# The last sums of a fused attention and feed-forward kernel: from GpSimd's only sum tile to VectorE and a tile of the scores' pool

## The chip, the cores and the metric

The kernel runs on one core of one Trainium2 chip. The metric is the device time of one execution in microseconds (us). The engines are called as the profile calls them: PE is TensorE (matmuls; PEld its weight loads), DVE is VectorE, ACT is ScalarE, POOL is GpSimd, and SP is the engine from whose queue most transfers (DMAs) are issued.

## The reference

```python
# q, k, v: (8, 8, 576, 64) float32; w_in: (512, 2048), w_out: (2048, 512)
scores = q @ k.transpose(0, 1, 3, 2) / sqrt(64)
kth = np.partition(scores, -32, axis=-1)[..., -32:-31]      # 32nd largest of each row
scores = np.where(scores >= kth, scores, -1e9)
attn = softmax(scores)                                       # over the last axis
x = (attn @ v).transpose(0, 2, 1, 3).reshape(4608, 512)
h = x @ w_in
out = (0.5 * h * (1 + erf(h / sqrt(2)))) @ w_out             # exact gelu
```

Attention with the 32 largest scores of each row kept, and a feed-forward layer with an exact gelu on the 4608 tokens that come out of it.

## The kernel before, in words

One program in float32 interleaves two stages, and the order of the instructions on every engine is written out by hand, as a loop over steps `n` with calls in a fixed order. An engine executes its instructions in that order. Semaphores are derived from which tile an instruction reads and writes, and from when a tile's slot was last used.

*Attention* works on 144 items of 128 rows by 1152 scores (two heads or halves of heads side by side). For an item, PE makes the scores (L370), ACT copies them into a tile of the scores' pool (tag `s`, six slots in turn), DVE finds the 32nd largest (L450, L453), ACT makes the exponentials (L495, L496), POOL divides by the sum (L507), PE turns the tile over (L553) and multiplies by `v` (L615). The result goes into `xT`.

*The feed-forward layer* works on "units": 256 tokens and two of the 16 blocks of 128 hidden columns (`FT` = 16). Units are taken in pairs, and `NU` is their number, so that `NU - 2` is the first unit of the last pair. For a pair, `first_block` makes `h` on PE (16 matmuls, L673), `gelus` applies the gelu on ACT into a tile `g` (L689, two slots), and `second_block` multiplies by `w_out`. Blocks are ordered so that `second_block` of a pair comes behind `first_block` of the next pair. At the end of the program no `first_block` is left, and so `second_block(NU - 4)` is followed at once by `second_block(NU - 2)`.

`second_block` is a product of 2 x 2 blocks made with seven multiplications instead of eight (the Strassen-Winograd scheme). It needs sums of the quarters of `g`, which `sums` makes: s1, s2 and s4 go into a tile `sum` that has one slot, and a third addition overwrites a quarter of `g` itself. The block starts with the seventh product (`seven_piece`, two matmuls, L809), whose operand is the quarter of `g` that the third addition has overwritten; then come three pairs of products, `TRIO = ((1, 2), (6, 5), (4, 3))`, 12 matmuls in all on L811 (four to a pair of products), which read `g`, `sum`, `w_out_sb` and `w_sum`. The seventh product is copied by ACT (L827, L830) and added up by POOL in `y7` (L832).

After the last block of a token group the products are combined into the output. For the last group of all, `last_parts` does so, called once after each pair of products (k = 0, 1, 2): for k = 0 ACT copies product 1 (L887); for k = 1 DVE makes five additions (L893 to L899) of which the second, L894, adds product 2 to product 1 and is stored at once (L895); for k = 2 come two more (L901, L903). Four stores of 128 x 256 float32 (128 KB) end the program: three on SP's queue (L895, L898, L902), one on ACT's (L904).

```python
dve(y0[:, B2], a[:, 0], y0[:, B1], op=add)                        # L893
dve(y0[:, B1], end_of["a"][:, 1], y0[:, B1], op=add)              # L894
nc.sync.dma_start(out=out[last_row : last_row + P, B1], in_=y0[:, B1])
dve(s7, s7, y0[:, B2], op=add)                                    # L896
```

`part_tile()` gives one of three slots of 128 x 256 float32, which the group before uses as well.

Of the kernel before, what the change touches and what calls it, by code (L numbers as in the profile page):

```python
# [14 lines left out]
def kernel(  # L15
# [19 lines left out]
    nc = tc.nc  # L35
    f32, i32, u32 = mybir.dt.float32, mybir.dt.int32, mybir.dt.uint32
    bf16, i16, u16 = mybir.dt.bfloat16, mybir.dt.int16, mybir.dt.uint16
    AF = mybir.ActivationFunctionType
    ALU = mybir.AluOpType

    B, H, S, D = q.shape
    P = 128
# [20 lines left out]
    work = ctx.enter_context(tc.tile_pool(name="work", bufs=2))  # L63
# [589 lines left out]
    NU = len(units)  # L653
    B1, B2 = slice(0, HALF), slice(HALF, DM)
# [43 lines left out]
    def sums(u):  # L698

        g = g_of[u].rearrange("p x (f n) -> p x f n", f=2)  # L700
        a11, a21, a12, a22 = (g[:, :, f, h * P : (h + 1) * P] for f in range(2) for h in range(2))
        t = work.tile([P, 2, 3, P], f32, tag="sum", bufs=1, name="sum")
        s1, s2, s4 = (t[:, :, x] for x in range(3))
        nc.gpsimd.tensor_tensor(s1, a21, a22, op=ALU.add)
        nc.gpsimd.tensor_tensor(s2, s1, a11, op=ALU.subtract)
        nc.gpsimd.tensor_tensor(a21, a11, a21, op=ALU.subtract)
        nc.gpsimd.tensor_tensor(s4, a12, s2, op=ALU.subtract)
        sums_of[u] = t

    def weight_sums(j):  # L710
# [29 lines left out]
    def y_tile():  # L740
        return work.tile([P, DM], f32, tag="y", name="y")

    def part_tile():
        return work.tile([P, HALF], f32, tag="part", bufs=3, name="part")
# [89 lines left out]
    end_of = {}  # L834

    def trio_piece(u, names, x):
# [8 lines left out]
        if u + x == NU - 1 or (end_of.get("last") and u + 2 == NU):  # L845
            last_parts(tok, k, a)
            return
# [34 lines left out]
    def last_parts(tok, k, a):  # L882

        dve, add = nc.vector.tensor_tensor, ALU.add
        if k == 0:
            end_of["y"] = y0, y1 = y_tile(), y_tile()
            nc.scalar.copy(out=y0[:, B1], in_=a[:, 0])  # L887
            end_of["a"] = a
            return
        y0, y1 = end_of["y"]  # L890
        s7 = y7[0]
        if k == 1:
            dve(y0[:, B2], a[:, 0], y0[:, B1], op=add)  # L893
            dve(y0[:, B1], end_of["a"][:, 1], y0[:, B1], op=add)  # L894
            nc.sync.dma_start(out=out[last_row : last_row + P, B1], in_=y0[:, B1])  # L895
            dve(s7, s7, y0[:, B2], op=add)  # L896
            dve(y1[:, B2], a[:, 1], s7, op=add)
            nc.sync.dma_start(out=out[last_row + P : last_row + 2 * P, B2], in_=y1[:, B2])  # L898
            dve(y0[:, B2], a[:, 1], y0[:, B2], op=add)  # L899
            return  # L900
        dve(y0[:, B2], a[:, 1], y0[:, B2], op=add)  # L901
        nc.sync.dma_start(out=out[last_row : last_row + P, B2], in_=y0[:, B2])  # L902
        dve(y1[:, B1], s7, a[:, 0], op=ALU.subtract)  # L903
        nc.scalar.dma_start(out=out[last_row + P : last_row + 2 * P, B1], in_=y1[:, B1])  # L904

    last_row = NT - TL - 2 * P
# [32 lines left out]
    def run_small(room):  # L939

        while summing:
            sums(summing.pop(0))
            room -= 4
        while small and room > 0:
            n, f = small.pop(0)
            f()
            room -= n
# [69 lines left out]
    first = {2: (0, 1, 1), 3: (2, 2, 3)}  # L1017
    prep_in, squares_in = {}, {}
    for pair in range(2, n_pairs):
        b, p = divmod(pair, NP)  # L1020
# [147 lines left out]
```

## Time and profile before

| | us |
|---|---|
| runs (three) | 1553.4, 1556.66, 1557.61 |
| median of the runs | 1556.66 |
| profiled execution, its own time | 1557.3 |
| span of the profiled execution, first to last instruction | 1555.5 |
| mean granted PE clock | 0.994 |

| engine | busy us | share of the span |
|---|---|---|
| PE | 1522.8 | 98% |
| DVE | 1330.3 | 86% |
| ACT | 1165.3 | 75% |
| POOL | 1141.5 | 73% |

All times in a trace count from the span's start. A line of the timeline gives the start, the duration (for a merged row of several instructions from the first start to the last end), the engine, the line of the kernel, and the tiles written and read; "[2.43 <-POOL g L706]" means that the engine stood idle for 2.43 us before it and that POOL's instruction on L706 ended that. The chain of waits is followed back from the last instruction, each step to what released it. The profile has two records for each of these float32 matmuls, so that `seven_piece` stands as x4 and a block's L811 as x24. The granted clock is the share of its full rate that PE was given in a window.

### The profile page before, as it was taken

What the parts mean: (1) busy time and instruction counts of PE and PEld (TensorE: products, weight loads), DVE (VectorE), ACT (ScalarE), POOL (GpSimd) and SP (SyncE); (2) the same over time, 40 slices, a digit from 0 to 9 for tenths busy, and PEclk for the clock granted to TensorE, in tenths of its full rate; (3) what the DMA queues carried; (4) which work ended last, traced back from release to release, by engine and by line L of the source; (5) the groups of instructions that cost most, each with busy time, mean ns of one, the idle gap of its engine ahead of it and who ended that gap; (6) DMA issues with size and microseconds to landing.
All of it is one profiled execution on the core that took longest, in us unless ns stands there. A gap on an engine that the chain in (4) does not pass through costs nothing. (4 is left out here: it accounts for less than half of the span.)

```text
span 1555.5 us, 28139 instructions
## 1 busy us (share of the span) xinstructions
PE 1522.8 (98%) x9280; PEld 1199.5 (77%) x9280; DVE 1330.3 (86%) x4571; ACT 1165.3 (75%) x2050; POOL 1141.5 (73%) x1291
## 2 busy tenths in 40 slices
PE   7899999999999999999999999999999999999998
PEld 5676578877777778887777778787877777787887
DVE  8998799989999988998989997988998998988700
ACT  6998877767777777777777778777777777777720
POOL 4886567767787868777787877776788786877632
PEclk9999999999999999999999999999999999999999
DMA  6513210012101111012201111002110111000000
GB/s 180 158 61 117 89 45 1 1 37 54 24 15 31 35 26 31 1 30 42 39 18 16 30 31 45 1 23 36 34 24 22 24 30 32 15 1 15 7 14 14
DMA packets 185298, 56.35 MB, mean 36 GB/s; under 512 B 176161, under 2 KB 176705, under 8 KB 185153
## 3 DMA queue, kind: packets, MB, share of 16 engines
q1 hardware_dynamic: 183888, 54.13, 14.6%
q8 instruction: 73, 1.20, 0.3%
q14 instruction: 73, 0.59, 0.1%
q10 hardware_dynamic: 1200, 0.39, 0.1%
q0 software_dynamic: 64, 0.03, 0.0%
HBM read 45.08 MB, written 9.44 MB: 35 GB/s over the span
## 5 line engine op out<-in xcount | busy, mean ns | idle before, releaser
L673 PE MATMUL h_ps<-xT,w_in_sb 128*128 128x256 f32 (+1 forms) x2560 | 541.4, 362 | 1.9 <-ACT xT L620 1.9
L673 PEld LDWEIGHTS h_ps<-xT,w_in_sb 128*128 128x128 f32 x2560 | 435.4, 191 | 73.4 <-issue 25.3
L450 DVE MAX8 top<-lists 128x8 f32<-128x288 f32 x792 | 321.1, 447 | 0.0
L507 POOL TENSOR_TENSOR s<-s,rden 128x1152 f32<-128x1152 f32 x144 | 302.7, 2102 | 0.3 <-DVE rden L482 0.3
L496 ACT ACTIVATE s<-s,bias 128x576 f32<-128x576 f32 x288 | 223.3, 775 | 11.9
L453 DVE MATCH_REPLACE8 lists<-top,lists 128x288 f32<-128x288 f32 x528 | 229.8, 443 | 0.0
L495 ACT ACTIVATE s<-s,neg 128x576 f32<-128x576 f32 x288 | 225.7, 784 | 2.8 <-POOL neg L475 2.7
L450 DVE MAX8 low<-lists 128x8 f32<-128x288 f32 x528 | 213.1, 445 | 0.0
L574 ACT COPY pt<-tp 128x1024 f32<-128x1024 f32 x133 | 134.8, 1014 | 96.1 <-PE tp L553 96.1
L488 POOL TENSOR_SCALAR den<-den 128x2 f32<-128x2 f32 x144 | 31.4, 218 | 236.0 <-ACT s L496 232.1
L421 POOL TENSOR_TENSOR lists<-lists 128x576 int32<-128x576 int32 x132 | 186.3, 1411 | 4.0
L413 POOL TENSOR_TENSOR lists<-s 128x576 int32<-128x576 int32 x132 | 185.6, 1406 | 0.0
L553 PE MATMUL tp<-ident,s 128*128 128x128 f32 x1152 | 150.7, 274 | 7.7 <-POOL s L507 7.7
L553 PEld LDWEIGHTS tp<-ident,s 128*128 128x128 f32 x1152 | 133.7, 141 | 27.3 <-POOL s L507 14.0
L615 PE MATMUL o<-pt,raw_v 128*64 128x256 f32 x1280 | 154.1, 386 | 0.4 <-ACT pt L560 0.4
L615 PEld LDWEIGHTS o<-pt,raw_v 128*64 128x64 f32 x1280 | 86.9, 137 | 87.0 <-issue 44.7
L475 POOL TENSOR_SCALAR neg<-kth 128x2 f32<-128x2 f32 x132 | 85.6, 649 | 88.3 <-DVE kth L466 88.3
L482 DVE RECIPROCAL rden<-den 128x2 f32<-128x2 f32 x144 | 23.4, 162 | 139.8 <-POOL den L488 138.6
L811 PE MATMUL y_ps<-w_out_sb,sum 128*128 128x256 f32 x480 | 142.8, 379 | 0.0
L378 ACT ACTIVATE s<-s_ps 128x1024 f32<-128x1024 f32 x127 | 124.3, 1025 | 15.7 <-PE s_ps L370 15.5
L370 PE MATMUL s_ps<-kt,qm 64*128 64x512 f32 x512 | 131.2, 626 | 0.8 <-ACT s L376 0.8
L453 DVE MATCH_REPLACE8 lists<-low,lists 128x288 f32<-128x288 f32 x264 | 114.9, 443 | 0.0
(148 smaller groups left out, 2784.1 us busy)
## 6 DMA issues: line engine op xcount, KB each, us to landing
raw_v<-in_v_dram SPq DMA_DIRECT2D x64, 128.0 KB, 2.4
out_dram<-y SPq DMA_DIRECT2D x30, 256.0 KB, 2.1
w_out_sb<-in_moe_w_in_dram SPq DMA_DIRECT2D x14, 511.8 KB, 4.9
raw_q<-in_q_dram SPq DMA_DIRECT2D x96, 64.0 KB, 2.0
raw_k<-in_k_dram SPq DMA_DIRECT2D x96, 64.0 KB, 2.0
w_out_sb<-in_moe_w_out_dram SPq DMA_DIRECT2D x10, 511.8 KB, 4.1
w_sum<-in_moe_w_out_dram SPq DMA_DIRECT2D x6, 511.8 KB, 4.1
raw_q<-in_q_dram SPq DMA_DIRECT2D x96, 8.0 KB, 1.8
```

Of the source, the lines that this page charges most:

```text
L413: nc.gpsimd.tensor_tensor(t[:, 1].bitcast(i32), a.bitcast(i32), b.bitcast(i32), op=ALU.add)
L421: nc.gpsimd.tensor_tensor(both, both, top, op=ALU.subtract)
L450: nc.vector.max(x[:, e], src[:, e])
L453: nc.vector.match_replace(dst[:, e], x[:, e], src[:, e], LOWEST)
L495: nc.scalar.activation(s, s, func=AF.Prelu, bias=st["neg"][:, e : e + 1], scale=1.0, alpha=STEEP)
L496: nc.scalar.activation(s, s, func=AF.Exp, bias=st["bias"][:, e : e + 1], scale=1.0, accum_out=st["den"][:, e : e + 1],)
L507: nc.gpsimd.tensor_tensor(s, s, wide, op=ALU.mult)
L553: nc.tensor.transpose(tp[:, j * P : (j + 1) * P], s[:, first + j * P : first + (j + 1) * P], ident)
L574: nc.scalar.copy(out=pt_now[0][:, 0 : 2 * NM, x : x + P], in_=tp.rearrange("p e (j n) -> p (e j) n", j=NM),)
L615: nc.tensor.matmul(o[e * D : (e + 1) * D, 0:n], lhsT=vt[:, j, e, :], rhs=pt[:, e * NM + j if j < NM else 2 * NM, :], start=(j == 0), stop= ...
L673: nc.tensor.matmul(h_tile(u)[:, i, :], lhsT=w_in_sb[:, ko, f * P : (f + 1) * P], rhs=xT[:, ko, c0 : c0 + n], start=(ko == 0), stop=(ko == ...
L811: nc.tensor.matmul(acc[names][:, k], lhsT=lhsT, rhs=rhs, start=(j == 0 and k == 0), stop=(j == FT // 2 - 1 and k == 1),)
```

## The change

In `sums`, the last pair of units (`u == NU - 2`) takes its sum tile from the scores' pool (tag `s`, a slot of 128 x 1152 float32, of which the first 768 columns are used) and makes the four additions on DVE. All other pairs keep POOL and the tile `sum`. In `last_parts`, the addition of products 1 and 2 moves from k = 1 to k = 0, goes into a part tile instead of over `y0`, and is stored from there; its store stays the first of the four, on the same queue. All other instructions keep their order on every engine; only the line numbers behind `sums` grow by six.

```diff
         a11, a21, a12, a22 = (g[:, :, f, h * P : (h + 1) * P] for f in range(2) for h in range(2))
-        t = work.tile([P, 2, 3, P], f32, tag="sum", bufs=1, name="sum")
+        if u == NU - 2:
+            t = work.tile([P, 2 * S], f32, tag="s", bufs=6, name="sum_s")
+            t = t[:, 0 : 6 * P].rearrange("p (x k n) -> p x k n", x=2, k=3)
+            add = nc.vector.tensor_tensor
+        else:
+            t = work.tile([P, 2, 3, P], f32, tag="sum", bufs=1, name="sum")
+            add = nc.gpsimd.tensor_tensor
         s1, s2, s4 = (t[:, :, x] for x in range(3))
-        nc.gpsimd.tensor_tensor(s1, a21, a22, op=ALU.add)
-        nc.gpsimd.tensor_tensor(s2, s1, a11, op=ALU.subtract)
-        nc.gpsimd.tensor_tensor(a21, a11, a21, op=ALU.subtract)
-        nc.gpsimd.tensor_tensor(s4, a12, s2, op=ALU.subtract)
+        add(s1, a21, a22, op=ALU.add)
+        add(s2, s1, a11, op=ALU.subtract)
+        add(a21, a11, a21, op=ALU.subtract)
+        add(s4, a12, s2, op=ALU.subtract)
         sums_of[u] = t
...
         if k == 0:
             end_of["y"] = y0, y1 = y_tile(), y_tile()
             nc.scalar.copy(out=y0[:, B1], in_=a[:, 0])
-            end_of["a"] = a
+            first = part_tile()
+            dve(first, a[:, 1], y0[:, B1], op=add)
+            nc.sync.dma_start(out=out[last_row : last_row + P, B1], in_=first)
             return
         y0, y1 = end_of["y"]
         s7 = y7[0]
         if k == 1:
             dve(y0[:, B2], a[:, 0], y0[:, B1], op=add)
-            dve(y0[:, B1], end_of["a"][:, 1], y0[:, B1], op=add)
-            nc.sync.dma_start(out=out[last_row : last_row + P, B1], in_=y0[:, B1])
             dve(s7, s7, y0[:, B2], op=add)
```

## The prediction

> **What bounds the kernel now.** I read the page's first part, then the chain of waits in order of time, then the timeline of the last 30 us, because both edits act on the last pair of units alone.
>
> ```profile
> span 1555.5 us, 28139 instructions
> PE 1522.8 (98%) x9280; PEld 1199.5 (77%) x9280; DVE 1330.3 (86%) x4571; ACT 1165.3 (75%) x2050; POOL 1141.5 (73%) x1291
> ```
>
> TensorE (PE) is busy for 98% of the span: whatever moves the end must take away time in which PE stands or runs slowly, or shorten what follows its last matmul. The chain of waits (start, us, engine, tile, line) shows where the end leaves PE:
>
> ```profile
> 1535.78 5.20 PE y_ps L811 x24
> 1541.13 0.73 POOL sum L704
> 1541.93 0.72 POOL sum L705
> 1542.65 0.69 POOL g L706
> 1543.39 1.13 PE seven L809 x4
> 1544.52 5.15 PE y_ps L811 x16
> 1549.85 0.44 DVE y L893
> ```
>
> So there are two places: three POOL additions between the last two blocks of PE, and the DVE additions after the last one. The timeline around the first place (start, duration, engine, line):
>
> ```profile
> 1534.75 1.03 PE L809 MATMUL seven<-w_sum,g 128*128 128x256 f32 x4
> 1535.03 1.09 ACT L689 ACTIVATE g<-h_ps 128x512 f32<-128x512 f32 x2 [11.60 <-PE h_ps L673]
> 1535.61 1.89 PE L811 MATMUL y_ps<-w_out_sb,g 128*128 128x256 f32 x8
> 1538.63 0.59 PE L811 MATMUL y_ps<-w_out_sb,sum 128*128 128x256 f32 x2
> 1539.93 0.59 PE L811 MATMUL y_ps<-w_sum,g 128*128 128x256 f32 x2
> 1540.36 0.59 PE L811 MATMUL y_ps<-w_out_sb,sum 128*128 128x256 f32 x2
> 1541.13 0.72 POOL L704 TENSOR_TENSOR sum<-g 128x256 f32<-128x256 f32 x1 [9.38 <-PE y_ps L811]
> 1542.61 0.72 POOL L706 TENSOR_TENSOR g<-g 128x256 f32<-128x256 f32 x1
> 1543.39 1.13 PE L809 MATMUL seven<-w_sum,g 128*128 128x256 f32 x4 [2.43 <-POOL g L706]
> 1544.35 3.25 PE L811 MATMUL y_ps<-w_out_sb,g 128*128 128x256 f32 x8
> 1549.06 0.59 PE L811 MATMUL y_ps<-w_out_sb,sum 128*128 128x256 f32 x2
> 1550.79 0.59 PE L811 MATMUL y_ps<-w_out_sb,sum 128*128 128x256 f32 x2
> ```
>
> The gelus are finished at 1535.03 + 1.09 = 1536.12, yet the sums of them start at 1541.13: POOL waited 9.38 us for PE, because there is one sum tile and PE reads it to the end of the block before. PE then stands for 2.43 us until the third addition (L706, which overwrites g) is done. A block of this kind takes 1540.36 - 1534.75 = 5.61 us from its first matmul to its last pair (the last row of x2); the last block takes 1550.79 - 1543.39 = 7.40. The windows (PE, PEld, DVE, ACT, POOL busy, granted PE clock, DMA) say why:
>
> ```profile
> 1543.40:1545.00 1.60, 1.60 (x7) 1.39 (x8) 0.00 (x0) 0.27 (x1) 1.30 (x2) 0.91 0.00 0
> 1545.00:1548.00 3.00, 3.00 (x9) 2.37 (x8) 0.00 (x0) 0.46 (x2) 0.72 (x1) 0.50 0.00 0
> ```
>
> The granted clock is 0.50 from 1545 to 1548, after the gap. It is not the only gap that a drop follows:
>
> ```profile
> 110.47 0.70 PE L673 MATMUL h_ps<-xT,w_in_sb 128*128 128x256 f32 x2 [1.86 <-ACT xT L620]
> 112.00:113.00 1.00, 1.00 (x3) 0.76 (x3) 0.63 (x4) 1.00 (x3) 0.33 (x2) 0.50 0.00 0
> ```
>
> Here a gap of 1.86 us is followed within 2 us by a clock of 0.50.
>
> **Term 1, the gap: -2.6 us.** The last sums go to DVE and into a slot of the scores' pool, which has six slots and whose last items were turned over long before. As built, the first addition's wait on PE is for a matmul 292 before the last one, so it starts with the gelus' end. The DVE additions of the tail give its price:
>
> ```profile
> 1549.85 0.42 DVE L893 TENSOR_TENSOR y<-y_ps,y 128x256 f32<-128x256 f32 x1 [70.56 <-PE y_ps L811]
> 1550.31 0.42 DVE L894 TENSOR_TENSOR y<-y_ps,y 128x256 f32<-128x256 f32 x1
> 1550.65 0.41 DVE L896 TENSOR_TENSOR y<-y,y 128x256 f32<-128x256 f32 x1
> 1551.10 0.42 DVE L897 TENSOR_TENSOR y<-y_ps,y 128x256 f32<-128x256 f32 x1
> 1551.44 0.41 DVE L899 TENSOR_TENSOR y<-y_ps,y 128x256 f32<-128x256 f32 x1
> 1551.96 0.42 DVE L901 TENSOR_TENSOR y<-y_ps,y 128x256 f32<-128x256 f32 x1
> 1552.30 0.41 DVE L903 TENSOR_TENSOR y<-y,y_ps 128x256 f32<-128x256 f32 x1
> ```
>
> DVE is empty when the gelus end: L893 ended an idle time of 70.56 us. The nearest row for an addition of two 128x256 SBUF tiles is L896. Start to start is 0.34 us where an addition doesn't need the one before (L894 to L896) and 0.45 where it does (L896 to L897). Of the four sums the second and fourth need the one before: 0.45 + 0.34 + 0.45 + 0.41 = 1.65 us, done by about 1537.9. At POOL's price of 0.72 each, which I take as the upper bound, it is 2.9 us, done by 1539.1. PE would reach the last block at 1540.36 + 0.43 = 1540.79 (0.43 is the step from 1539.93 to 1540.36). The cover is 1.7 to 2.9 us, so the sums cost nothing. If it were gone, each us that the third addition ends after 1540.8 is a us of PE. PE's gain is 1543.39 - 1540.79 = 2.60; if the change from one block to the next costs a pipeline's end as the chain has it (1535.78 + 5.20 = 1540.98), 2.41.
>
> **Term 2, the clock: -1.8 us.** Without a gap the last block should take 5.61 as the block before, not 7.40: 1.79 less. Its last pair then starts at 1540.79 + 5.61 = 1546.40 in place of 1550.79, 4.39 earlier for both terms. The bounds are 0 (the drop stays, or a typical run doesn't have it) and 1.79, and I take the upper, because two gaps of this size are both followed by a drop. The Trainium skill, "TensorE: Matmul & The Clock Gate", section "HAM oscillation — how this bites in real kernels", puts the limit at gaps over about 3.4 us, by which a 2.43 us gap would bring no drop and the sum would lack this term. The trace doesn't agree: 0.50 behind gaps of 2.43 and 1.86 us.
>
> **Term 3, the tail: -0.4 us.** L894 leaves the DVE's row of additions; it goes ahead, as an addition into a part tile that waits for the copy of the first trio. In the warm block that trio ends 1535.61 + 1.89 - 1534.75 = 2.75 us after the block's start, now 1543.54.
>
> ```profile
> 1547.65 0.37 ACT L887 COPY y<-y_ps 128x256 f32<-128x256 f32 x1 [2.54 <-PE y_ps L811]
> 1550.76 0.33 SPq L895 DMA_DIRECT2D out_dram<-y  x1
> 1552.74 0.37 ACTq L904 DMA_DIRECT2D out_dram<-y  x1
> out_dram<-y SPq DMA_DIRECT2D x3, 128.0 KB, 1.7
> out_dram<-y ACTq DMA_DIRECT2D x1, 128.0 KB, 1.8
> ```
>
> The copy (0.37) and the addition (0.42) end near 1544.4. Queued behind that addition on DVE is the one that waits for the second trio, whose last pair starts at 1540.79 + (1538.63 - 1534.75) = 1544.67; before, L893 began 0.79 after that pair (1549.06 to 1549.85), so now at 1545.46, a full us after the new addition has ended. Then follow three additions and the last two: by the steps of the rows 0.46, 0.45, 0.34, 0.52, 0.34 the last one starts at 1545.46 + 2.11 = 1547.57, against 1552.30: 4.73 earlier. PE asks for no more: its last pair at 1546.40 + 0.79 gives 1547.19, and the addition that needs it (L901 before) is due at 1547.23. Of L893's 0.20 us after the pair's end (1549.06 + 0.59), ACT's copy needs only 0.05 (1544.35 + 3.25 to 1547.65); as built, L893's waits for transfers stood partly behind its wait for PE and now stand ahead of it, worth up to 0.15. The sum is therefore -4.7 to -4.9, and I take **-4.8**.
>
> The store of the moved part is issued on SP near 1544.5 in place of 1550.76 and lands in about 1.7, before the other three are issued; they keep their order and their queues. The last store remains the one on ACT's queue, with its landing of 1.8, so I cost the early store at 0; the upper bound of its gain is the 0.1 by which the last one lands later than the median of the other three. POOL loses four additions; its last but one addition of a product, which followed them, comes some 7 us sooner, and nobody waits for that.
>
> The profiled execution took 1557.3 us, a span of 1555.5 and 1.8 around it, 0.6 above the median of the runs, 1556.66. The sum gives 1552.5 for it, and on the median **1551.9**. 0.3% of 1556.66 is 4.67, about what a measurement of this kernel can tell from no change; so the bound lies at 1551.99, a tenth of a us from the forecast.
>
> **Rivals.** (a) *The clock term isn't there.* If the typical run of before has no drop in its last block, or the drop stays, only 3.0 go: 1553.7. For it: the lowest run of before, 1553.4, lies 3.3 below the median, and two drops of 1.8 would make 3.6. Against it: the profiled run has both drops and lies with the two upper runs. The Trainium skill, same page, section "What's actually happening", says that the window of activity behind the clock runs freely, by which the same gap could bring a drop in one run and none in the next; no run here shows that. Chance 0.16.
>
> (b) *The sums don't start sooner*, because the first addition still waits for PE's last read. Then the third ends at 1541.13 + 0.45 + 0.34 + 0.41 = 1542.33 in place of 1542.61 + 0.72 = 1543.33: 1.0 from PE and 0.4 from the tail, 1555.3. Against it stands the place of the wait as built. Chance 0.06.
>
> (c) *DVE and POOL hold each other up*, and it gets slower. Two groups of the page bear on it:
>
> ```profile
> L488 POOL TENSOR_SCALAR den<-den 128x2 f32<-128x2 f32 x144 | 31.4, 218 | 236.0 <-ACT s L496 232.1
> L475 POOL TENSOR_SCALAR neg<-kth 128x2 f32<-128x2 f32 x132 | 85.6, 649 | 88.3 <-DVE kth L466 88.3
> L507 POOL TENSOR_TENSOR s<-s,rden 128x1152 f32<-128x1152 f32 x144 | 302.7, 2102 | 0.3 <-DVE rden L482 0.3
> ```
>
> L475 has the shape of L488 and takes three times as long; it runs beside a DVE operation on two SBUF tiles (L406). The place is DVE's queue from 1536.1 on. It decides against the change once the third sum ends after 1543.33 + 0.4, when it eats up the tail's gain too: 2.5 us for each of three additions. With two POOL operations of L507's length ahead of each, 3 x (0.42 + 4.2) = 13.9 us, PE would start at 1550.0, 6.6 later than now, and the time would be 1562.9. Against it: POOL has a single addition of 0.72 there, and one such delay stays under the cover of 1.7 us or more. The Trainium skill, "SBUF — State Buffer", section "Who interferes with whom", states that such DVE and GpSimd operations exclude each other for a whole instruction; L475 agrees. Chance 0.03.
>
> **How the numbers follow.** The whole sum has 0.75, and its time lies just beyond the bound, so I give 0.51 of that to faster and 0.24 to same. (a) is same (0.12), and faster where the scatter of runs helps (0.04); (b) is same; (c) is slower. That makes faster 0.55, same 0.42, slower 0.03. The range goes up to (a) and half a us beyond, 1554.2, and down by 2.2 from the forecast, since one run of before in three lies 3.3 below its median: 1549.7. Rival (b), (c) and the outermost runs are left out, under 2 in 10.
>
> **What would show it.** Right: four DVE additions near 1536.2 to 1538; the last block's first matmul without a wait on POOL or DVE; a granted clock of 1.00 to the last matmul, its last pair 5.6 us after the block's first; the last two additions some 0.25 us behind PE's last matmul (1550.79 + 0.59 to 1551.96 was 0.58), and the first store 2 us or more ahead of the second. Wrong: a wait "seven <- DVE" on PE, a clock of 0.50 in the last block, or DVE additions of over 0.8 us. A drop behind the gap at 108 us that is gone or stays would move the time by 1.7 with no part of the change in it.

## The result: 1552.86 us, and what the profile after shows

| | before | after |
|---|---|---|
| median of 18 runs each, us | 1556.53 | 1552.86 |
| lowest and highest, us | 1553.03, 1558.11 | 1550.03, 1553.32 |
| ratio, 95% interval | | 0.9979 (0.9971 to 0.9986) |
| span of the profiled execution, us | 1555.5 | 1551.1 |

The change gains 3.7 us by the medians and 2.2 to 4.5 us by the interval. That is 0.21% by the ratio: clear of zero, but less than 0.3%. Both profiled executions have the clock drop behind PE's gap near 108 us (before from 111.12 us, after from 110.68), so that drop is no part of the difference between them.

The chain of waits of the changed kernel (start, us, engine, tile, line) has no step on POOL at its end any more; one block of PE follows the other:

```profile
1535.29 0.86 PE seven L815 x4
1536.16 5.18 PE y_ps L817 x24
1541.34 0.86 PE seven L815 x4
1542.20 3.47 PE y_ps L817 x16
1545.69 0.43 DVE y L901
```

Its timeline around the two edits, to be held against the rows of the prediction:

```profile
1535.13 1.03 PE L815 MATMUL seven<-w_sum,g 128*128 128x256 f32 x4
1535.41 1.09 ACT L689 ACTIVATE g<-h_ps 128x512 f32<-128x512 f32 x2 [11.60 <-PE h_ps L673]
1536.53 0.43 DVE L710 TENSOR_TENSOR sum_s<-g 128x256 f32<-128x256 f32 x1 [56.86 <-ACT g L689]
1536.84 0.72 POOL L838 TENSOR_TENSOR y<-y,p 128x256 f32<-128x256 f32 x1 [4.70 <-ACT p L836]
1536.99 0.85 DVE L711 TENSOR_TENSOR sum_s<-sum_s,g 128x256 f32<-128x256 f32 x1
1537.77 0.41 DVE L712 TENSOR_TENSOR g<-g 128x256 f32<-128x256 f32 x1
1538.10 0.41 DVE L713 TENSOR_TENSOR sum_s<-g,sum_s 128x256 f32<-128x256 f32 x1
1541.17 1.03 PE L815 MATMUL seven<-w_sum,g 128*128 128x256 f32 x4
1544.37 0.42 DVE L895 TENSOR_TENSOR part<-y_ps,y 128x256 f32<-128x256 f32 x1 [5.86 <-ACT y L893]
1544.82 0.33 SPq L896 DMA_DIRECT2D out_dram<-part  x1
1545.69 0.42 DVE L901 TENSOR_TENSOR y<-y_ps,y 128x256 f32<-128x256 f32 x1 [0.90 <-PE y_ps L817]
1546.79 0.59 PE L817 MATMUL y_ps<-w_out_sb,sum_s 128*128 128x256 f32 x2
1547.54 0.42 DVE L907 TENSOR_TENSOR y<-y_ps,y 128x256 f32<-128x256 f32 x1
1547.88 0.41 DVE L909 TENSOR_TENSOR y<-y,y_ps 128x256 f32<-128x256 f32 x1
```

Counted from the first matmul of the block before the last (1534.75 before, 1535.13 after):

| | before | after | gain |
|---|---|---|---|
| last block starts | 8.64 | 6.04 | 2.60 |
| its last pair starts | 16.04 | 11.66 | 4.38 |
| last DVE addition starts | 17.55 | 12.75 | 4.80 |

The windows (PE, PEld, DVE, ACT, POOL busy, clock, DMA) show PE busy without a break and at full clock through both blocks:

```profile
1535.00:1541.00 6.00, 6.00 (x30) 5.28 (x29) 1.95 (x4) 1.35 (x3) 0.72 (x1) 1.00 0.00 0
1541.00:1547.30 6.30, 6.30 (x30) 5.28 (x28) 1.90 (x5) 0.74 (x2) 0.73 (x1) 1.00 0.06 21
```

So between these two executions the sum of the prediction, 4.8, is found to a tenth. (Their spans differ by 4.4 only, because the block before the last began 0.38 later in the execution of the changed kernel.) The medians of the runs give 1.1 less than 4.8. The experiments ask where that went. Theory A: the clock drop is paid in only a part of the executions of before. Theory B: every execution pays it, and the change loses 1.1 to 1.5 us elsewhere. Five rounds were run of each kernel, beside runs of before on the same chip.

### The profile page after: what moved, and what is told of

Same layout as the page of the kernel before. It is cut to its first block, busy times and chain, and to the rows that moved or that the text cites. A ratio compares the mean times of both kernels' runs of the same rounds, so it can differ in the third digit from the quotient of the medians.

```text
span 1551.1 us, 28140 instructions
## 1 busy us (share of the span) xinstructions
PE 1520.4 (98%) x9280; PEld 1198.1 (77%) x9280; DVE 1332.4 (86%) x4575; ACT 1166.1 (75%) x2050; POOL 1140.2 (74%) x1287
```

## Experiments, first series: the parts and the gaps

Before in this series: median 1556.28, lowest 1552.90, highest 1557.56, mean 1556.04 (25 runs).

**The sums alone.** The new `sums` with the old `last_parts`:

```diff
-            first = part_tile()
-            dve(first, a[:, 1], y0[:, B1], op=add)
-            nc.sync.dma_start(out=out[last_row : last_row + P, B1], in_=first)
+            end_of["a"] = a
...
+            dve(y0[:, B1], end_of["a"][:, 1], y0[:, B1], op=add)
+            nc.sync.dma_start(out=out[last_row : last_row + P, B1], in_=y0[:, B1])
```

> The sums of the last pair on DVE in a tile of the scores' pool; the second addition of the tail stays where it was. Theory A (the sums give the gap's 2.6 us in every execution; the clock drop behind the gap is paid only in executions in which a free-running window of about 3.4 us falls badly on the gap, so its 1.8 us are saved in a part of them): in the trace no wait of PE ahead of the last block, clock 1.00 in it, last DVE addition 4.4 us earlier counted from the start of the block before (before 17.55, now 13.1 to 13.2); the lowest runs 2.6 below before's lowest of 1553.0, the median of all about 3.2 below. Theory B (the drop is paid in every execution of before, and the change loses 1.1 to 1.5 us elsewhere): the same trace, but all runs shifted alike, and with the early store left out the loss may be gone: 4.4 below.

Measured: median 1552.23 (1550.05 to 1553.38), mean 1552.19, ratio 0.9976 (0.9966 to 0.9985). The lowest is 2.85 below that of before, the mean 3.85. In the trace the last addition starts 13.07 us after the start of the block before, 0.3 later than in the changed kernel. The sums are nearly all of the change. The lowest run fell by 2.85, where A expects 2.6 and B 4.4 in every run, which speaks for A; the median fell by 4.05 where A had 3.2, and the interval, 2.3 to 5.3 us, holds both theories. The profile also shows something that was not looked for: PE's gap near 108 us is there, and no drop follows.

```profile
109.21 0.70 PE L673 MATMUL h_ps<-xT,w_in_sb 128*128 128x256 f32 x2 [1.85 <-ACT xT L620]
108.00:115.00 7.00, 5.79 (x30) 4.42 (x31) 6.42 (x25) 5.71 (x13) 5.75 (x7) 1.00 0.20 44
```

**The early store alone.** The new `last_parts` with the old `sums`:

```diff
-            end_of["a"] = a
+            first = part_tile()
+            dve(first, a[:, 1], y0[:, B1], op=add)
+            nc.sync.dma_start(out=out[last_row : last_row + P, B1], in_=first)
...
-            dve(y0[:, B1], end_of["a"][:, 1], y0[:, B1], op=add)
-            nc.sync.dma_start(out=out[last_row : last_row + P, B1], in_=y0[:, B1])
```

> The sums stay on POOL in the only sum tile; only the addition of products 1 and 2 and its store go ahead. Theory A: the last DVE addition 0.35 to 0.5 us earlier counted from the start of PE's last block, gap 2.43 and drop as before; time 0.4 below before, not to be told from no change (0.3% is 4.67 us, and five rounds tell perhaps 1 us). Theory B with the loss in the early store: time 0.7 to 1.1 above before.

Measured: median 1555.61 (1552.52 to 1557.23), ratio 0.9994 (0.9985 to 1.0003), not to be told from no change; no loss of 0.7 to 1.1 either, against B in that form. In the trace the last addition starts 6.87 us after the last block, against 7.22 with the old tail at the same clock (the next experiment): 0.35 earlier, as A expected. The main finding is elsewhere in the profile. The gap ahead of the last block is the same 2.43 us as in the profile of before, and the clock stays at 1.00 (the expectation had the drop in this trace, and missed):

```profile
1543.71 1.13 PE L809 MATMUL seven<-w_sum,g 128*128 128x256 f32 x4 [2.43 <-POOL g L706]
1545.00:1548.00 3.00, 3.00 (x16) 2.64 (x15) 0.42 (x1) 0.74 (x2) 0.74 (x2) 1.00 0.00 0
```

**The last gap filled.** The kernel before; PE multiplies the identity while it would stand:

```diff
         j = units[u][2] // 2
+        if u == NU - 2:
+            keep_busy(10, ident)
         seven[0] = bank("seven")
```

> The kernel before, with ten matmuls of the identity (0.22 us each, 2.2 us, result unused) between the last two blocks of PE, so that the gap stays in time but PE is busy in it: the clock term by itself. Theory A: the last block starts at the same distance from the block before (8.64 us), takes 5.6 in place of 7.4 us, clock 1.00; the lowest runs stay at before's lowest 1553.0 to 1553.4, the upper group (1556.4 to 1558.1) comes down by up to 1.8, the mean falls by about 0.8 to 1.2. Theory B: every run falls by 1.8, lowest runs near 1551.3.

Measured: median 1554.72 (1553.00 to 1556.19), mean 1554.63; ratio 0.9993 (0.9985 to 1.0002), which doesn't exclude no change. The last block starts at the same place (8.65 us after the block before) and PE waits 0.21 in place of 2.43:

```profile
1540.26 2.39 PE L997 MATMUL warm<-ident 128*128 128x128 f32 x20
1542.87 1.13 PE L809 MATMUL seven<-w_sum,g 128*128 128x256 f32 x4 [0.21 <-POOL g L706]
1545.00:1548.00 3.00, 3.00 (x16) 2.64 (x15) 0.36 (x1) 0.37 (x1) 0.38 (x1) 1.00 0.00 0
```

The lowest run stays where before's is (1553.00 against 1552.90), and the highest falls by 1.4: as A expects, and not as B does, which wanted 1551.3 for the lowest. The mean falls by 1.4, of the 1.8 that the prediction gave a drop, but the interval, from 2.3 us faster to 0.3 slower, is wider than the effect.

**The other gap filled, in the changed kernel.**

```diff
         for ko in range(part * KO // m, (part + 1) * KO // m):
+            if u == 0 and x == 1 and ko == KO - 1:
+                for _ in range(8):
+                    nc.tensor.matmul(
+                        h_tile(1)[:, 0, 0:P], lhsT=ident, rhs=ident, start=True, stop=True
+                    )
```

> The changed kernel, with eight matmuls of the identity (0.22 us each, 1.75 us, result unused) in PE's gap at 108.5 to 110.4 us, the other gap that a clock drop follows. Theory A: no drop behind it in any execution, so that the two groups of the changed kernel's runs (1550.0 to 1550.3, and 1552.4 to 1553.3) come closer: upper group down by up to 1.7 to about 1551.3, lower group stays at 1550.2; trace without a clock under 1.00 from 108 to 116. Theory B: every run falls by 1.7, the lowest to 1548.4.

Measured: 1551.09 (1549.76 to 1551.20), ratio to before 0.9968 (0.9955 to 0.9980). Four of the five runs, at 1550.83 to 1551.20, lie 1.9 below the upper group of the changed kernel; the fifth, 1549.76, lies only 0.3 below the lowest run there, and not 1.7: this speaks for A, on five runs.

```profile
111.00:115.00 4.00, 4.00 (x24) 2.98 (x22) 3.41 (x13) 3.09 (x8) 2.77 (x5) 1.00 0.15 34
```

## Experiments, second series: tile or engine, and the scatter

Before in this series: median 1556.36 (29 runs).

**POOL in the scores' pool.**

```diff
             t = t[:, 0 : 6 * P].rearrange("p (x k n) -> p x k n", x=2, k=3)
-            add = nc.vector.tensor_tensor
+            add = nc.gpsimd.tensor_tensor
```

> As the changed kernel, but the four sums of the last pair stay on POOL; only their tile comes from the scores' pool. Theory A (what counts is that the sums need not wait for the only tile; the engine does not matter): sums from 1536.1 to 1539.1 by the times of the profile of before, no wait of PE ahead of the last block, the last DVE addition as early as with DVE's sums (12.75 us after the start of the block before, at most 0.1 off); time as the changed kernel's within 0.6. Theory C (the engine matters, the sums on POOL are too late): PE waits in the last block and the time is 1 us or more above the changed kernel's.

Measured: 1552.48 (1549.76 to 1553.13), ratio 0.9978 (0.9968 to 0.9987), as good as DVE's (0.9979). The last addition starts 12.80 us after the block before, within the 0.1 that A allowed.

```profile
1536.51 0.72 POOL L710 TENSOR_TENSOR sum_s<-g 128x256 f32<-128x256 f32 x1 [4.44 <-ACT g L689]
1538.68 0.73 POOL L713 TENSOR_TENSOR sum_s<-g,sum_s 128x256 f32<-128x256 f32 x1
1541.11 1.03 PE L815 MATMUL seven<-w_sum,g 128*128 128x256 f32 x4
```

The sums are done at 1539.4, and PE starts its block at 1541.11 without a wait. It is the tile that counts; once the sums have it, the engine makes no difference.

**DVE in the only sum tile.**

```diff
-            t = work.tile([P, 2 * S], f32, tag="s", bufs=6, name="sum_s")
-            t = t[:, 0 : 6 * P].rearrange("p (x k n) -> p x k n", x=2, k=3)
+            t = work.tile([P, 2, 3, P], f32, tag="sum", bufs=1, name="sum")
             add = nc.vector.tensor_tensor
```

> As the changed kernel, but the sums on DVE go into the only sum tile, so that they wait for PE's last read of it. Theory A: gap of PE about 1.4 us in place of 2.43, last block 1.0 us earlier than in the kernel before counted from the block before (7.6 in place of 8.64), and a clock drop behind it in fewer executions or none: the time 1.4 below before without a drop, up to 3.2 where before has one. Theory C: as the changed kernel.

Measured: 1553.49 (1551.29 to 1554.57), ratio 0.9986 (0.9977 to 0.9995), 1.0 above the kernel with POOL in the other tile. DVE now waits for PE's last read, and PE for DVE:

```profile
1540.08 0.42 DVE L709 TENSOR_TENSOR sum<-g 128x256 f32<-128x256 f32 x1 [61.80 <-PE y_ps L816]
1541.44 1.10 PE L814 MATMUL seven<-w_sum,g 128*128 128x256 f32 x4 [1.50 <-DVE g L711]
1542.00:1546.00 4.00, 4.00 (x20) 3.54 (x19) 0.42 (x1) 0.74 (x2) 0.72 (x1) 1.00 0.00 0
```

The gap is 1.50 and the block starts 7.71 us after the one before, 0.93 sooner than in before. So a faster engine alone is worth 0.9 us, the tile alone the whole 2.6; and this kernel behaves as rival (b) of the prediction has it.

**Before, with both gaps filled** (the edits of the two filled kernels above together):

> The kernel before with matmuls of the identity in both gaps (eight at 108 us, ten ahead of the last block; results unused). Beside the changed kernel with the gap at 108 us filled it shows what the change is worth where no clock drop can follow either gap. Theory A: 3.0 above that one (2.6 from the gap, 0.4 from the tail), median 1554.1, all runs within 2 us, no drop in the trace after 60 us. Theory B (1.1 to 1.5 us lost elsewhere in the change): 1.5 to 1.9 above it.

Measured: 1553.59 (1552.81 to 1554.41), 2.5 above the changed kernel with its gap filled by medians and 2.8 by means, in a scatter of 1.6 us; the last addition starts 15.87 us after the block before, there 12.75, a difference of 3.12. That lies nearer to A's 3.0 than to B's 1.5 to 1.9, but the two kernels were run in different series, and the scatter is too wide to settle it.

**The changed kernel, with the early gaps filled too.** To the filled gap at 108 us come

```diff
             copy(out=dst, in_=tp[:, 0 : len(group) * P])
+            if pair == 3 and c == 2:
+                keep_busy(19, ident)
...
-            keep_busy((4 if product or n == 0 else 14) * (1 if n < 5 else 2), ident)
+            keep_busy(16 if n == 0 else (4 if product else 14) * (1 if n < 5 else 2), ident)
```

> The changed kernel with the gap at 108 us filled as before, and two more gaps in which PE waits early in the program (twelve more matmuls of the identity at 16 us, nineteen at 43.7 us; results unused). Theory A: no granted clock under 1.00 from 15 us to the end in the trace, one group of runs, at or below the lowest runs of the changed kernel, 1549.5 to 1550.3. Theory B says nothing of the level; if the runs still fall into two groups, something other than the clock divides them.

Measured: 1549.64 (1549.44 to 1549.95), ratio to before 0.9961 (0.9948 to 0.9974): one group of runs, all of them below the lowest of the changed kernel. One drop is left, from 30.64 to 34.05 us, which the expectation (none from 15 us on) did not have. The long window behind it shows 1.00, but a single drop would vanish there in the rounding; it is the mean clock of the whole span, 0.999 of 1548.0 us, that leaves a loss of about 1.5 us, room for one drop and no second:

```profile
30.50:34.50 4.00, 4.00 (x22) 3.92 (x21) 4.00 (x15) 3.91 (x6) 4.00 (x4) 0.57 0.82 260
115.00:1500.00 1385.00, 1373.78 (x8377) 1079.93 (x8376) 1221.91 (x4214) 1061.26 (x1876) 1037.12 (x1181) 1.00 0.13 29
```

So it is PE's early gaps and the clock behind them that divide the runs of the changed kernel. For before, the record shows the clock's part without any filling: of its 77 runs in the three series the 18 lowest (up to 1554.14) have a mean granted clock of 0.996 to 0.999, and the 59 others (from 1555.66) of 0.993 to 0.996.

## Experiments, third series: each term without the scatter

With the early gaps filled the terms can be measured one by one. The edits are those above, combined.

> The kernel before with matmuls of the identity in all four gaps (16, 43.7 and 108 us, and the one ahead of the last block; results unused), so that the scatter of runs is gone. Against the changed kernel with its three gaps filled (run beside it), it gives the change without a clock term. Theory A: 3.0 to 3.1 above it, 1552.7, within 0.6 of each other. Theory B (1.1 to 1.5 lost elsewhere): 1.5 to 2.0 above.

> The sums alone on DVE, the tail as before, three early gaps filled. Theory A: 0.35 to 0.45 above the changed kernel with its gaps filled, 1550.0, that is 2.6 to 2.7 below the kernel before with all gaps filled. If the early store costs something, it lies below the changed kernel.

> The kernel before with the three early gaps filled and the gap ahead of the last block left as it is. What is left of the scatter is the clock drop behind that gap. Theory A: two groups of runs, one with the kernel before with all gaps filled (1552.7), the other 1.6 to 1.8 above it (1554.4), the upper with half to four fifths of the runs. Theory B (every execution pays): one group, 1554.4.

> The changed kernel with its three gaps filled once more (16, 43.7 and 108 us; results unused), as the reference on the same chip for the other three. Expected 1549.4 to 1550.0 in one group.

| early gaps filled in all | runs | median us | lowest, highest |
|---|---|---|---|
| before, last gap filled too | 12 | 1552.81 | 1552.37, 1553.67 |
| before, last gap as it was | 11 | 1552.91 | 1552.63, 1554.96 |
| sums on DVE, old tail | 5 | 1550.11 | 1549.69, 1550.53 |
| the whole change | 5 | 1549.77 | 1549.40, 1550.22 |

The whole change is worth 1552.81 - 1549.77 = 3.04 us where the last gap is filled: 2.70 from the sums, 0.34 from the early store. A had expected 3.0 to 3.1; B, with 1.5 to 2.0, is out. (The kernel before with all gaps filled spreads over 1.3 us, where 0.6 was expected. The 0.34 is less than the spread of either row's five runs, 0.8, and rests on the traces: the last addition starts 13.06 us after the block before with the old tail, and 12.76 with the new one.) With the last gap left open, eight runs lie from 1552.63 to 1552.98, with those whose gap is filled, and three at 1554.23, 1554.29 and 1554.96, some 1.4 to 2.1 above. By its size that is one drop in three of eleven executions; none of the three has a trace, but their mean clocks, 0.998, 0.997 and 0.996, lie on that side of the eight's 0.998 and 0.999. The two groups were expected, the share (half to four fifths) was not. The profiled one belongs to the eight; same gap, full clock:

```profile
1540.70 1.13 PE L816 MATMUL seven<-w_sum,g 128*128 128x256 f32 x4 [2.43 <-POOL g L713]
1541.00:1544.00 3.00, 3.00 (x15) 2.64 (x14) 0.00 (x0) 0.74 (x2) 1.74 (x3) 1.00 0.02 5
```

## Why the prediction was right, and where it was off

*Range and sign* were right: 1552.86 lies in 1549.7 to 1554.2. The point, 1551.9, was 1.0 too low, and the likelier side of the bound (faster by over 0.3%) was not the one that came.

*Term 1, the gap, 2.6:* right, 2.60 in the traces and 2.70 in the runs without scatter. The sums on DVE ran from 1536.53 to 1538.51, 0.3 longer than the row-by-row sum, because L711 took 0.85 in place of 0.41; the cover held, with 2.7 us to spare. The first addition waited for ACT alone, so rival (b) didn't occur, and its price was near (1.50 us of gap where 1.4 was worked out). What the prediction put down to DVE and the pool together the pool's tile gives alone, with POOL making the sums.

*Term 3, the tail, 0.4:* right, 4.80 - 4.38 = 0.42 between the traces of before and after, 0.30 to 0.35 in pairs of traces that differ in the tail alone (13.06 - 12.76, 7.22 - 6.87), 0.34 in the runs. The new addition ended at 1544.79, 0.9 before the next one was due, as worked out. L893's extra 0.15 came off, since L901 starts 0.04 after the pair that it waits for (1545.69 against 1545.06 + 0.59 in the timeline); half of it went again in the step to the next addition, 0.53 in place of 0.46.

*Term 2, the clock, 1.8:* the mis-sized step. "I take the upper, because two gaps of this size are both followed by a drop" reads a rule out of one execution. Gaps of 2.43 us stand without a drop in two other profiles and the gap of 1.85 in a third. Per drop the size was nearly right. Behind the same 2.43 us gap the last block takes 7.40 us to its last pair with the drop and 5.72 without (1549.43 - 1543.71 in the early store alone, 1546.42 - 1540.70 in the third series), so the drop costs 1.68; the other 0.1 of the 1.79 is the slower first product behind the wait (1.13 in place of 1.03) and goes with the gap whatever the clock does. The groups of the third series lie 1.4 to 2.1 apart. The share of executions that pay it is not 1: the last gap filled alone gave 1.4 in the mean, with before's early gaps in place; three executions of eleven paid it with those filled; and in the 18 runs of the result it comes to 3.67 - 3.04 = 0.63 by the medians. Rival (a), with 0.16, was nearer to this than the main case: not "no drop in the typical run", but a drop in some, and the chance ought to have been split by the share. The three times of before at hand, one at 1553.4 and two at 1556.7 and 1557.6, already showed that not every execution pays the same, though not which gap makes the difference.

*Rival (c)* occurred in small: L838 on POOL ran from 1536.84 to 1537.56, and DVE's L711 beside it took twice its time. In five other profiles with the two side by side it took 0.85 or 0.86, and in the kernel with DVE in the only tile, where POOL ran nothing beside it, 0.43. The Trainium skill, "SBUF — State Buffer", section "Who interferes with whom", has the two exclude each other where both read from SBUF; the 0.85 against 0.41 agrees. With one such meeting the price was 0.4 us, under cover.

What sets the share of executions with a drop the traces show in part. In the profile of before the drops begin at 18.96, 46.27, 111.12 and 1544.72 us, which are 8, 19 and 420 steps of 3.413 us apart; the other profiles keep the same step, but their grids lie differently against the start of the span. So the same gap falls differently into the windows of the grid. The rows (PE busy, clock, DMA) give two such windows each of the kernel before, of the early store alone, and of before with the early gaps filled, around the same gap of 2.43 us:

```profile
1541.31:1544.72 3.41, 1.33 (x6) 1.00 0.00 0
1544.72:1548.13 3.41, 3.41 (x10) 0.50 0.00 0
1541.97:1545.38 3.41, 1.67 (x8) 1.00 0.00 0
1545.38:1548.79 3.41, 3.41 (x18) 1.00 0.11 37
1535.98:1539.40 3.42, 2.29 (x11) 1.00 0.00 0
1539.40:1542.81 3.41, 2.11 (x10) 1.00 0.02 5
```

Where PE was busy for 1.33 us of a window, the next one had half the clock; with 1.67 us, or with the gap divided between two windows, it had the full clock. The limit is not sharp: behind the gap near 108 us windows with 1.56 us came out both ways (no drop with the sums alone, a drop with DVE in the only tile), and early in the program a window with 1.71 us was followed by a drop (before with all gaps filled, at 27.46). The Trainium skill, "TensorE: Matmul & The Clock Gate", section "What's actually happening", has a window that runs freely beside the kernel; the same 2.43 us with 0.50 once and 1.00 twice agree with it. The same page's rule that only gaps over about 3.4 us matter (section "HAM oscillation — how this bites in real kernels") doesn't hold here. What stays open is how often the grid lies badly. The four fifths by the mean of one kernel and the three of eleven of another, which differ in their early gaps, are not shown to differ: the interval of the first reaches from none to all.

## What to carry to other kernels

Before moving work to another engine, look for what it waits for: here the tile with one slot held the sums back 5 us, and a second slot alone, with the same engine, gave the same gain. A price read behind a gap in one profiled execution (a clock drop) is a price with a probability; the groups into which the runs fall show how often it is paid, and kernels with the gap filled by matmuls whose result nobody reads measure it. The same filling is a tool for measuring small changes: it took the scatter of before from 5 us (18 runs) to 1.3 (12 runs), and of the changed kernel from 3.3 (18 runs) to 0.8 (ten runs in two series).

## What the runs showed of the hardware that was not expected

A clock drop lasts 3.41 us or twice that. The first three of the profile of before (PE busy, clock, DMA):

```profile
18.96:22.37 3.41, 3.41 (x11) 0.50 0.42 91
46.27:53.10 6.83, 5.25 (x18) 0.50 0.80 233
111.12:114.53 3.41, 3.41 (x14) 0.50 0.00 0
```

At half the clock a drop of 3.41 us costs at most 1.7 us, and the last block of before lost 1.68. A drop comes behind gaps of PE as short as 1.86 us (before, at 110.47) and fails to come behind longer ones of 2.43. Matmuls whose result nobody reads made the program faster: 1549.64 with the gaps filled, the fastest version of this study, against 1552.86 for the changed kernel.
